# Logits matmuls in groups of forty, and the last block evacuated by VectorE with the residual added there

## The chip, the cores and the metric

One core of a Trainium2 chip. The metric is the device time of one execution in microseconds (us). Every execution shown here is fast, at a granted TensorE clock of 0.998 or more, unless it is a single look. Quoted times are medians. Ratios are the mean time of one kernel's fast runs over the mean of the kernel before's fast runs of the same rounds on the same chip, so they are not quite the ratio of the quoted medians.

## The reference

A layer norm without weights feeds two branches whose results are added to the input:

```python
xn = _layernorm(x)                       # x: 1 x 2048 x 640, bf16
return x + _A_ref(xn, wqkv, wo) + _B_ref(xn, w1, b1, w2, b2)
# A: 32 heads of 20; each position attends to 8 positions, 0, 2, .. 14 back
#    logits = sum_d q[s,d] * k[s - 2w, d];  softmax over w;  o = sum_w attn * v;  o @ wo
# B: gelu(xn @ w1 + b1) @ w2 + b2         # hidden width 1536
```

## The kernel before

The 2048 positions are worked in four chunks of 512. VectorE multiplies q with shifted k (two of the eight shifts make one product of 128 x 2 x 5 x 512). TensorE sums the 20 elements of each head with a matrix of zeros and ones, `head_of`, into the logits L. The four blocks of 128 positions go to four strips of 32 columns of the array, so each of these matmuls has the form 128*32.

```python
def do_lg(n, wp):                                   # one product: 20 matmuls
    prod = tiles["qk", n, wp]
    for t in range(KT):                             # 5
        for j in range(BPC):                        # 4 strips
            nc.tensor.matmul(L[j*H:(j+1)*H, 2*wp:2*wp+2, :], lhsT=head_of[:],
                             rhs=prod[:, :, t, j*P:(j+1)*P], ...)
    ...                                             # chunk 0: the mask
```

After the softmax, the weights `attn` (32 heads on 128 rows) are copied to the four rows that hold each head's 20 elements (4 rows of 5) by transfers into one buffer `ax`, two blocks issued from the SP queue and two from ScalarE's queue:

```python
axp = ctx.enter_context(tc.tile_pool(name="axp", bufs=1))
def do_xd(n): expand(nc.sync, n, (0, 1))
def do_xs(n): expand(nc.scalar, n, (2, 3))          # stands in ScalarE's queue
```

ScalarE empties the four PSUM buffers into which TensorE writes projections and the hidden layer. The last block of the output gets its residual by an identity matmul, and its two halves are copied out by ScalarE (lo, 512 columns) and VectorE (hi, 128 columns):

```python
if pc == 3 and n * BPC + bl == LASTB:
    srcs.append((ident[:], x_sb[:, n * BPC + bl, :]))
...
nc.scalar.copy(osb[:, 0:CH], tiles["lo", *last][:])                    # do_oclo
nc.sync.dma_start(out_sd[LASTB * P :, 0:CH], osb[:, 0:CH])
nc.vector.tensor_copy(osb[:, CH:D], tiles["hi", *last][:, 0 : D - CH]) # do_ochi
nc.scalar.dma_start(out_sd[LASTB * P :, CH:D], osb[:, CH:D])
```

A small list scheduler, run when the kernel is built, orders some 550 pieces on the engines by ranks; hand-searched offsets to these ranks stand in the table `RANK`.

## Time and profile before

| | before |
|---|---|
| time, median of 5 (range) | 218.71 us (218.47 to 218.94) |
| TensorE, VectorE, ScalarE busy | 97%, 83%, 51% of the span |
| share of TensorE in the chain that ended last | 93% |
| first projection matmul starts | 7.39 us |
| last evacuation (hi) starts | 213.65 us |
| from there to the end of the span | 3.00 us |

I call the time from the first projection to the last evacuation the stream: 213.65 - 7.39 = 206.26 us. It is the part that the change touches. In front of it are the first loads, behind it the last stores. The tail before, in the timeline:

```profile
212.64 0.59 ACT L676 CAST osb<-lo 128x512 bf16<-128x512 f32 x1 [1.89 <-issue]
...
213.25 0.36 SPq L677 DMA_DIRECT2D out_dram<-osb  x1
213.65 0.29 DVE L685 CAST osb<-hi 128x128 bf16<-128x128 f32 x1 [14.05 <-PE hi L657]
213.98 0.36 ACTq L686 DMA_DIRECT2D out_dram<-osb  x1
```

The columns are start, duration, engine, line, operation, output and input, and in brackets the idle time before and what ended it.

### The profile page before, as it was taken

How to read it: one execution, taken by the hardware profiler on the slowest of the kernel's cores; microseconds unless marked ns; L12 is line 12 of the kernel's file. 1: busy time of each engine (PE TensorE's matmuls, PEld its weight loads, DVE VectorE, ACT ScalarE, POOL GpSimd, SP SyncE). 2: the span in 40 equal slices, each digit the busy share in tenths (PEclk: the TensorE clock that was granted, in tenths of full speed). 3: DMA queues.
4: the chain of work that ended last, by engine and by line, in shares of the span. 5: the costliest groups of instructions: out<-in, count | busy, mean ns of one | idle time of the engine just before them, and what ended most of it. 6: DMA issues, size and time to landing. Idle time of an engine off the chain costs nothing.

```text
span 216.7 us, 3977 instructions
## 1 busy us (share of the span) xinstructions
PE 209.4 (97%) x1689; PEld 121.1 (56%) x1714; DVE 180.2 (83%) x169; ACT 110.6 (51%) x195; POOL 14.5 (7%) x33
## 2 busy tenths in 40 slices
PE   7899999999999999999999999999999999999994
PEld 7799855554554555555555455554544555555552
DVE  3759999988999999999899999989999999922000
ACT  3665999796757554734184625026665311341211
POOL 2000000000000000101010101011010011101121
PEclk9999999999999999999999999999999999999999
DMA  6999931907314401336020280222025222200253
GB/s 221 366 365 393 375 136 48 259 0 185 72 30 118 97 0 44 77 57 170 3 30 0 30 193 3 30 33 29 2 33 107 87 30 33 28 2 3 30 61 62
DMA packets 18761, 20.83 MB, mean 96 GB/s; under 512 B 6328, under 2 KB 15928, under 8 KB 18744
## 3 DMA queue, kind: packets, MB, share of 16 engines
q1 hardware_dynamic: 15144, 15.83, 24.7%
q0 software_dynamic: 2160, 2.46, 9.4%
q10 hardware_dynamic: 1440, 2.29, 3.1%
q8 instruction: 13, 0.21, 0.4%
q14 instruction: 4, 0.03, 0.0%
HBM read 10.00 MB, written 5.08 MB: 70 GB/s over the span
## 4 chain that ended last, share of the span: by engine, by line
PE 93%; DVE 1%; ACT 1%; DMA 1%; ACTq 1%; issue 1%; DVEq 0%
PE lo L655 27%; PE pps L455 23%; PE hps L622 22%; PE gps L472 8%; PE hi L657 8%; PE L L517 5%; DMA x_sb<-in_A_x_dram 1%; PE tp L416 1%; ACTq L584 1%; ACT L633 1%; DVE stats L375 0%; DVE stats L376 0%; ACT xnT L420 0%; ACT hT L633 0%; DVE xn L402 0%
## 5 line engine op out<-in xcount | busy, mean ns | idle before, releaser
L622 PE MATMUL hps<-xnT,w_sb 128*128 128x512 bf16 x230 | 53.2, 379 | 0.4
L655 PE MATMUL lo<-w_sb,hT 128*128 128x512 bf16 x187 | 52.9, 379 | 0.0
L505 DVE TENSOR_TENSOR prod<-qT,kT 128x2560 bf16<-128x2560 bf16 x32 | 45.4, 1483 | 0.7 <-ACT kT L490 0.7
L600 DVE TENSOR_TENSOR pv<-vT,ax 128x2560 bf16<-128x2560 bf16 x32 | 45.7, 1484 | 0.0
L657 PE MATMUL hi<-w_sb,hT 128*128 128x128 bf16 x192 | 40.3, 219 | 0.5 <-issue 0.3
L622 PEld LDWEIGHTS <-w_sb 128*128 128x128 bf16 x240 | 22.8, 98 | 26.3 <-issue 0.2
L633 ACT ACTIVATE hT<-hps,b1T 128x512 bf16<-128x512 f32 x48 | 31.4, 686 | 11.8 <-PE hps L622 9.8
L662 ACT CAST osb<-lo 128x512 bf16<-128x512 f32 x15 | 8.8, 586 | 53.8 <-PE hi L657 35.4
L609 DVE TENSOR_TENSOR pv<-pv 128x5120 bf16<-128x5120 bf16 x12 | 33.9, 2823 | 0.3
L655 PEld LDWEIGHTS <-hT 128*128 128x128 bf16 x192 | 18.7, 98 | 23.0 <-issue 1.5
L668 POOL DMA_DIRECT2D out_dram<-osb x15 | 13.1, 873 | 196.8 <-ACT osb L663 196.8
L655 PE MATMUL lo<-wo,oT 128*128 128x512 bf16 x75 | 22.1, 379 | 0.0
L657 PEld LDWEIGHTS <-hT 128*128 128x128 bf16 x192 | 18.4, 98 | 1.8
L455 PE MATMUL pps<-xnT,wv_sb 128*128 128x512 bf16 x74 | 17.3, 379 | 0.3 <-ACT hT L633 0.2
L657 PE MATMUL hi<-wo,oT 128*128 128x128 bf16 x80 | 16.9, 219 | 0.3
L455 PE MATMUL pps<-xnT,wk_sb 128*128 128x512 bf16 x74 | 16.8, 379 | 0.1
L455 PE MATMUL pps<-xnT,wq_sb 128*128 128x512 bf16 x72 | 16.7, 379 | 0.2
L490 ACT CAST vT<-pps 128x512 bf16<-128x512 f32 x15 | 8.7, 586 | 11.4 <-PE pps L455 9.4
L655 PEld LDWEIGHTS <-oT 128*128 128x128 bf16 x80 | 7.8, 98 | 9.6 <-issue 0.4
L455 PEld LDWEIGHTS <-wk_sb 128*128 128x128 bf16 x75 | 8.7, 118 | 7.3 <-issue 0.2
L455 PEld LDWEIGHTS <-wq_sb 128*128 128x128 bf16 x75 | 8.6, 118 | 7.1
L455 PEld LDWEIGHTS <-wv_sb 128*128 128x128 bf16 x75 | 8.5, 118 | 7.3 <-issue 0.5
(67 smaller groups left out, 208.9 us busy)
## 6 DMA issues: line engine op xcount, KB each, us to landing
w_sb<-in_B_w_dram SPq DMA_DIRECT2D x2, 1920.0 KB, 16.2
out_dram<-osb POOLq DMA_DIRECT2D x15, 160.0 KB, 3.4
ax<-attn SPq DMA_DIRECT2D x8, 256.0 KB, 4.9
ax<-attn ACTq DMA_DIRECT2D x8, 256.0 KB, 5.6
x_sb<-in_A_x_dram SPq DMA_DIRECT2D x3, 640.0 KB, 11.2
out_dram<-x_sb SPq DMA_DIRECT2D x3, 640.0 KB, 3.9
wq_sb<-in_A_wqkv_dram SPq DMA_DIRECT2D x1, 800.0 KB, 5.2
wk_sb<-in_A_wqkv_dram SPq DMA_DIRECT2D x1, 800.0 KB, 7.3
```

What stands on the lines that cost most here:

```text
L455: nc.tensor.matmul(ps[:], lhsT=wqkv_p[which][:, ti, to, :], rhs=xnT[:, ti, :], start=(ti == 0), stop=(ti == KT - 1),)
L472: nc.tensor.matmul(ps[:, i, :], lhsT=wqkv_p[which][:, ti, to, :], rhs=tiles["xnT", 0][:, ti, cs], start=(ti == 0), stop=(ti == KT - 1),)
L505: nc.vector.tensor_tensor(out=prod[:, i, :, :], in0=qkv_tile(n, 0)[:], in1=qkv_tile(n, 1)[:, :, off : off + CH], op=ALU.mult,)
L517: nc.tensor.matmul(L[j * H : (j + 1) * H, 2 * wp : 2 * wp + 2, :], lhsT=head_of[:], rhs=prod[:, :, t, j * P : (j + 1) * P], start=(t == 0 ...
L600: nc.vector.tensor_tensor(out=pv[:, i, :, :].rearrange("p t (j c) -> p t j c", j=BPC), in0=qkv_tile(n, 2)[:, :, off : off + CH].rearrange( ...
L609: nc.vector.tensor_tensor(out=ta[:], in0=ta[:], in1=tb[:], op=ALU.add)
L622: nc.tensor.matmul(ps[:], lhsT=w1_sb[:, ti, ft * P : (ft + 1) * P], rhs=tiles["xnT", n][:, ti, :], start=(ti == 0), stop=(ti == KT - 1),)
L633: nc.scalar.activation(hT[:], tiles["hps", n, ft][:], ACT.Gelu_apprx_tanh, bias=b1T[:, ft : ft + 1], scale=1.0)
L655: nc.tensor.matmul(lo[:], lhsT=lhs, rhs=rhs[:, 0:CH], start=first, stop=last)
L657: nc.tensor.matmul(hi[:, 0 : D - CH], lhsT=lhs, rhs=rhs[:, CH:D], start=first, stop=last)
L662: nc.scalar.copy(osb[:, 0:CH], tiles["lo", n, bl][:])
L668: nc.gpsimd.dma_start(rows, tiles["osb", n, bl][:], accum_op=ALU.add)
```

## The change

Its intent is to take work out of TensorE's stream: one group of forty logits matmuls instead of two of twenty, so that TensorE changes its tiling half as often, and no identity matmul for the last block's residual. The ranks were searched anew, so the order of all pieces differs.

```diff
-RANK = { "ad00": 178, "av2": 376.9, "f11": 47.4, ... }
+RANK = { "av2": 6.5, "f11": 4.6, "f12": 35.6, ... }
...
-            pl.add(f"lg{n}{wp}", PE, 0.65, ..., [pr, L], slack=0.8)
+            if wp % 2:
+                both = [("prod", "qk", n, wp - 1), pr]
+                pl.add(f"lg{n}{wp}", PE, 1.2, ..., both + [L], slack=0.8)
...
     def do_lg(n, wp):
-        prod = tiles["qk", n, wp]
+        for x in range(2):
+            prod = tiles["qk", n, wp - 1 + x]
+            logits(L, prod, wp - 1 + x)
...
-            if pc == 3 and n * BPC + bl == LASTB:
-                srcs.append((ident[:], x_sb[:, n * BPC + bl, :]))
...
-        nc.scalar.copy(osb[:, 0:CH], tiles["lo", *last][:])
+        nc.vector.tensor_tensor(out=osb[:, 0:CH], in0=tiles["lo", *last][:], in1=x_sb[:, LASTB, 0:CH], op=ALU.add)
...
-        nc.vector.tensor_copy(osb[:, CH:D], tiles["hi", *last][:, 0 : D - CH])
+        nc.vector.tensor_tensor(out=osb[:, CH:D], in0=tiles["hi", *last][:, 0 : D - CH], in1=x_sb[:, LASTB, CH:D], op=ALU.add)
```

## The prediction

> **What bounds the kernel now.** I read the views in this order: the page's busy shares and slices, the chain that ended last, the waits of TensorE, the timeline around one group of logits matmuls, and the timeline of the tail.
>
> The busy shares and the slices come first, because they say whether there is one bound or a sequence of them.
>
> ```profile
> PE 209.4 (97%) x1689; PEld 121.1 (56%) x1714; DVE 180.2 (83%) x169; ACT 110.6 (51%) x195; POOL 14.5 (7%) x33
> ...
> PE   7899999999999999999999999999999999999994
> ...
> PEclk9999999999999999999999999999999999999999
> ```
>
> TensorE is busy in every slice between the ramp and the tail, at a clock that is never held back. VectorE at 83% is next, and must be watched. A busy TensorE alone proves little, since it can be busy with rows that wait; the chain settles it.
>
> ```profile
> PE 93%; DVE 1%; ACT 1%; DMA 1%; ACTq 1%; issue 1%; DVEq 0%
> PE lo L655 27%; PE pps L455 23%; PE hps L622 22%; PE gps L472 8%; PE hi L657 8%; PE L L517 5%; DMA x_sb<-in_A_x_dram 1%; PE tp L416 1%; ACTq L584 1%; ACT L633 1%; DVE stats L375 0%; DVE stats L376 0%; ACT xnT L420 0%; ACT hT L633 0%; DVE xn L402 0%
> ```
>
> The chain is TensorE's own instruction stream for 93% of the span. The logits matmuls (L L517) are 5% of it. The waits of TensorE, all of them:
>
> ```profile
> PE idle L694 <- POOL ident masks.py:199: 1.6, 1, 1.6
> PE tp L416 <- DVE xn L402: 0.5, 1, 0.5
> PE hi L657 <- issue: 0.3, 2, 0.2
> PE gps L472 <- ACT xnT L420: 0.2, 1, 0.2
> PE pps L455 <- ACT hT L633: 0.2, 1, 0.2
> ```
>
> Only 0.2 us of these (pps on ACT) is waiting for another engine after the ramp; the first projection starts at 7.39 us. So from 7.39 us to the end of the matmuls at about 213.5 us the time is a sum of matmul pitches, and what this change takes out of TensorE's stream comes out of the time one for one, unless it opens a wait. From the starts in the trace, the pitches are 216 ns for 512 columns and 55.5 ns for 128.
>
> Now one group of logits matmuls, between two streams of 512 columns:
>
> ```profile
> 53.81 0.81 PE L455 MATMUL pps<-xnT,wv_sb 128*128 128x512 bf16 x3
> 54.55 0.73 PE L517 MATMUL L<-prod,head_of 128*32 128x256 bf16 x20
> 55.21 0.39 PE L655 MATMUL lo<-w_sb,hT 128*128 128x512 bf16 x1
> 55.44 0.22 PE L657 MATMUL hi<-w_sb,hT 128*128 128x128 bf16 x1
> ```
>
> The third pps matmul starts at 54.24; the first logits matmul starts 0.31 us later instead of 0.22. The lo matmul starts at 55.21. What is inside the group shows when the same timeline is cut to ever longer beginnings of another group:
>
> ```profile
> 92.74 0.29 PE L517 MATMUL L<-prod,head_of 128*32 128x256 bf16 x4
> ...
> 92.74 0.40 PE L517 MATMUL L<-prod,head_of 128*32 128x256 bf16 x8
> ...
> 92.74 0.51 PE L517 MATMUL L<-prod,head_of 128*32 128x256 bf16 x12
> ```
>
> Four matmuls (the four blocks of 32 columns of the array) run side by side, and each further round of four adds 0.11 us. A group of twenty is five rounds, 0.55 us; the rest is paid once per group, however long it is.
>
> **What the Trainium skill says.** "TensorEngine Tiling (Array Packing)", Key Properties, says that changing the tiling mode drains TensorE, while moving between tiles of one mode does not. The form 128*32 in the rows is such another mode, and the trace agrees: round to round costs 99 to 110 ns from start to start, but into and out of the mode there are holes. "TensorE: Matmul & The Clock Gate", The mechanism, has tiles in different columns starting about 4 ns apart; the trace has 3 to 4 ns between the four of a round. The same page, Back-to-back issue gap, gives about 131 ns per matmul at 512 columns as a sustained rate and 215.7 ns isolated; here the sustained pitch is 216 ns, so I use the trace. "VectorE: DVE Perf Modes", the perf-mode tier table, has tensor_tensor at one element per cycle with a PSUM operand; the trace agrees in the subtraction from the logits, 1224 ns for 1024 elements.
>
> **The change part by part.**
>
> *Groups of forty.* The fixed cost of a group, from the starts in the trace, over all sixteen groups: entering 309 - 216 = 93 ns behind 512 columns, and 149 - 55 = 94 ns behind 128; the first round takes 109 instead of 99 ns, 10; from the last round to the next foreign matmul 205 instead of 99 ns, 106; the first foreign matmul 226 instead of 216, 10. Sum 220 ns. Check: from the pps at 54.24 to the second foreign matmul at 55.44 there are 1.20 us; less 0.216 for each of the two foreign 512-column matmuls leaves 0.765, less 5 rounds of 0.109 leaves 0.22. The built order of the changed kernel has eight groups (41, 41 and six of 40 matmuls, the two of 41 with the mask), never adjacent, for sixteen. It saves 8 x 0.220 = 1.76 us. Rounds, weight loads and mask matmuls are as many as before.
>
> *Identity matmul.* Two matmuls leave the last block's chain, lo and hi from x_sb: 0.216 + 0.055 = 0.27 us, both on the path, the tail being TensorE's.
>
> *Last evacuation.* The lo half moves from ScalarE (586 ns) to VectorE. Estimate from the 1224 ns row: 1024 elements at 0.96 GHz are 1067 ns, so 157 ns fixed, and 512 elements 0.69 us. Before, the lo copy started at 212.64 and the hi copy at 213.65, 1.01 us apart; with one hi matmul fewer, 0.95 us. So VectorE has finished lo (0.69 us) before hi arrives, and nothing is added. The hi add is 128/0.96 + 157 = 0.29 us, and the copy it replaces took 0.292. The lo store is issued 0.1 us later, but the hi store still comes after it. Net zero.
>
> *The new order.* The ranks are new, so everything is reshuffled. Two things count. The transpose of b1 moves behind the load of its input, for which TensorE's loader waited 0.2 us: about -0.1. ScalarE loads activation tables 11 times instead of 9, 2 x 1283 ns more on an engine that is 51% busy.
>
> Sum: -1.76 - 0.27 - 0.1 = -2.13 us. I give 0.15 us back for small new waits in an order whose every wait I cannot check: 218.56 - 2.0 = about 216.6 us, 0.9% less.
>
> **Rivals.**
>
> *A group of forty waits for VectorE.* It needs four products before its first matmul where it needed two, and two of the four product buffers stay full until it ends. One product late by 1.4 us in every group would be 8 x 1.4 = 11 us, and the kernel would be slower. Against it: no logits matmul of the kernel before waited at all, and the order gives TensorE other work first. First group: TensorE passes 35 hps matmuls (7.6 us) and 5 transposes (0.3) after the projections that ended at 25.2, so it arrives near 33.1. VectorE began the products at 23.32; it now has one statistics block (1.0) and one scaling more ahead, so about 24.6, plus 4 x 1.40 = 30.2. Second group: TensorE 33.1 + 1.44 + 15 transposes (0.85) + 20 matmuls (4.3) = 39.7; VectorE 24.6 + 9 x 1.40 (eight products, one bias add) = 37.2. Both have over 2 us to spare. If one later group did wait, I would expect 0.3 to 1 us, not 11.
>
> *VectorE's end becomes the bound.* The last bias add (1.40 us) moves from the middle of VectorE's stream almost to its end, and its store, on which the last four accumulating stores build, goes out late. Before, VectorE idled 7.35 us before the last oT, so it can take 1.4 us more there. Two additions of 2.74 us follow the bias add, so it ends some 5.5 us before VectorE's free point of 190.8; the store takes about 3 us, and the first of those accumulating stores went out at 199 or later. It is hidden: zero.
>
> *ScalarE evacuates late.* Four PSUM buffers carry projections and hidden layer; a table load (1.28 us) at a bad place can hold TensorE. The trace shows 0.2 us of this for nine loads. Two more, fully exposed, would eat 2.6 us and leave the time where it was or 0.5 us above.
>
> *The switch is not what costs.* If the 220 ns were the loading of weights, which stays, merging would save nothing and only 0.27 us would be left (218.3). Against it: the weight loader idles 5.5 us before 15 of the groups and hardly elsewhere, which is what a drain looks like.
>
> **Range and chances.** The two sure terms give 216.5. Full exposure of one table load, or a late product or two, gives 217.6; an order a little tighter than before, which can win only the few tenths TensorE still waits, gives 215.9. I take 215.8 to 217.7. Two per cent is 4.4 us, twice what the removed work is worth, and there is no further idle time on TensorE after 7.39 us to win; 2% slower needs 6.4 us of new waits. Faster by over 2%: 0.02; within 2%: 0.95; slower: 0.03.
>
> **What would show each step right or wrong.** Right: eight groups with x40 or x41 in the timeline, the next foreign matmul 1.2 us after the first logits matmul; the loader's idle time before logits at about half of 5.5 us; no rows lo or hi from x_sb and ident; TensorE busy near 207.4 us; the lo add near 0.69 us and done before the hi add begins. Wrong: a wait of an L row on prod in TensorE's waits; pps or hps waiting on ACT rows for more than 1 us; groups that last 1.5 us (the cost scales with matmuls); or a first projection that no longer starts at 7.4 us, which I took as unchanged.

## More of the kernel before

```profile
123.89 2.30 ACTq L584 DMA_DIRECT2D ax<-attn  x2
126.23 0.59 ACT L490 CAST vT<-pps 128x512 bf16<-128x512 f32 x1 [2.00 <-issue]
```

Two issues hold ScalarE's queue for 2.30 us, and the evacuation behind them waits. TensorE did not wait for it there.

## The result, and the profile after

The changed kernel takes 218.34 us (217.94 to 218.39, five runs) against 218.71: ratio 0.998, 95% interval 0.9965 to 0.9995. The gain is real and tiny, 0.4 us where 2.0 were predicted, and the time lies outside the predicted range. Busy shares and chain after:

```profile
PE 208.2 (96%) x1689; PEld 122.4 (57%) x1712; DVE 181.1 (84%) x170; ACT 111.4 (51%) x196; POOL 14.5 (7%) x33
...
PE 59%; DVE 32%; ACTq 2%; ACT 2%; issue 2%; DMA 1%; DVEq 0%
```

TensorE is busy 1.2 us less, and it no longer carries the whole chain: a third of the span now leads through VectorE, and ScalarE's queue (ACTq) has 2%. Each group of forty, here one between streams of 512 columns, is as predicted:

```profile
94.98 0.81 PE L458 MATMUL pps<-xnT,wk_sb 128*128 128x512 bf16 x3
95.72 1.28 PE L534 MATMUL L<-prod,head_of 128*32 128x256 bf16 x40
96.93 0.41 PE L458 MATMUL pps<-xnT,wk_sb 128*128 128x512 bf16 x1
```

The foreign matmul comes 1.21 us after the first of the forty, as the prediction asked. From the starts in the trace, entering still costs 309 ns instead of 216 and leaving 205 instead of 99. The weight loader's idle time in front of logits, in its view of waits before and after, halves with the number of groups:

```profile
PEld L517 <- issue: 5.5, 15, 0.4
```

```profile
PEld L534 <- issue: 3.0, 8, 0.4
```

What came in its place is in the waits of TensorE after the change:

```profile
PE pps L458 <- ACT vT L493: 0.8, 1, 0.8
...
PE pps L458 <- ACT hT L640: 0.5, 1, 0.5
```

From start to start these two cost 0.93 us (at 131 us) and 0.69 us (at 55 us). The waits view shows less, since it counts from the modelled ends of the matmuls. Around the one at 131 us the timeline shows three engines:

```profile
122.70 5.69 DVE L607 TENSOR_TENSOR pv<-vT,ax 128x2560 bf16<-128x2560 bf16 x4
122.92 4.48 PE L458 MATMUL pps<-xnT,wv_sb 128*128 128x512 bf16 x20
...
128.43 2.32 ACTq L591 DMA_DIRECT2D ax<-attn  x2
...
130.79 2.05 ACT L493 CAST vT<-pps 128x512 bf16<-128x512 f32 x4 [6.93 <-issue]
131.43 1.02 PE L458 MATMUL pps<-xnT,wv_sb 128*128 128x512 bf16 x4 [0.77 <-ACT vT L493]
```

TensorE fills the four PSUM buffers (20 matmuls) by 127.4 us. ScalarE should empty them, but in its queue the issues of the third chunk's expansion stand first. They may not start before VectorE has read the old contents of `ax`, at 128.4, and then take 2.3 us. Before the change the same issues left at 123.89, because VectorE was 4.5 us earlier there. The wait at 55 us stands behind the first chunk's pair of issues, with a table load of ScalarE between (first in ScalarE's view, then in that of all engines):

```profile
50.85 2.44 ACTq L591 DMA_DIRECT2D ax<-attn  x2
...
53.94 1.28 ACT L640 ACT_TABLE_LOAD   x1
55.23 1.27 ACT L640 ACTIVATE hT<-hps,b1T 128x512 bf16<-128x512 f32 x2
```

```profile
54.21 1.24 PE L458 MATMUL pps<-xnT,wq_sb 128*128 128x512 bf16 x5
...
55.97 1.24 PE L458 MATMUL pps<-xnT,wq_sb 128*128 128x512 bf16 x5 [0.52 <-ACT hT L640]
```

The tail after:

```profile
212.50 0.69 DVE L681 TENSOR_TENSOR osb<-lo,x_sb 128x512 bf16<-128x512 f32 x1 [16.09 <-PE lo L660]
...
213.21 0.35 SPq L682 DMA_DIRECT2D out_dram<-osb  x1
213.39 0.29 DVE L690 TENSOR_TENSOR osb<-hi,x_sb 128x128 bf16<-128x128 f32 x1 [0.20 <-PE hi L662]
213.71 0.36 ACTq L693 DMA_DIRECT2D out_dram<-osb  x1
```

The stream is 213.39 - 7.63 = 205.76 us, only 0.50 shorter. The first projection started 0.24 us later, and the end, after the hi add, is 0.15 us longer. The store of the lo half, from issue to landing, before and after (last column, us; the hi store, which lands last, takes 1.69 instead of 1.53):

```profile
out_dram<-osb SPq DMA_DIRECT2D x1, 128.0 KB, 1.7
```

```profile
out_dram<-osb SPq DMA_DIRECT2D x1, 128.0 KB, 2.0
```

### The profile page after: what moved, and what is told of

The parts are those of the page before. It is cut to its first block, busy times and chain, and to the rows that moved or that the text cites. A ratio compares the mean times of both kernels' runs of the same rounds, so it can differ in the third digit from the quotient of the medians.

```text
span 216.5 us, 3974 instructions
## 1 busy us (share of the span) xinstructions
PE 208.2 (96%) x1689; PEld 122.4 (57%) x1712; DVE 181.1 (84%) x170; ACT 111.4 (51%) x196; POOL 14.5 (7%) x33
## 4 chain that ended last, share of the span: by engine, by line
PE 59%; DVE 32%; ACTq 2%; ACT 2%; issue 2%; DMA 1%; DVEq 0%
PE lo L660 19%; PE hps L629 18%; DVE pv L607 10%; DVE prod L508 9%; PE gps L475 8%; PE pps L458 5%; PE hi L662 5%; DVE pv L616 5%; PE L L534 2%; ACTq L591 2%; DVE ssum L569 2%; DMA x_sb<-in_A_x_dram 1%; DVE attn L581 1%; DVE m L547 1%; PE tp L419 1%
## 5 line engine op out<-in xcount | busy, mean ns | idle before, releaser
L629 PE MATMUL hps<-xnT,w_sb 128*128 128x512 bf16 x232 | 54.5, 379 | 0.5
L458 PE MATMUL pps<-xnT,wv_sb 128*128 128x512 bf16 x73 | 16.6, 379 | 0.8 <-ACT vT L493 0.8
L681 DVE TENSOR_TENSOR osb<-lo,x_sb 128x512 bf16<-128x512 f32 x1 | 0.7, 692 | 16.1 <-PE lo L660 16.1
L378 DVE BATCH_NORM_STATS2 stats<-x_sb 128x6 f32<-128x320 bf16 x16 | 7.4, 463 | 7.6 <-DMA x_sb<-in_A_x_dram 7.5
```

What stands on the lines that cost most here:

```text
L458: nc.tensor.matmul(ps[:], lhsT=wqkv_p[which][:, ti, to, :], rhs=xnT[:, ti, :], start=(ti == 0), stop=(ti == KT - 1),)
L629: nc.tensor.matmul(ps[:], lhsT=w1_sb[:, ti, ft * P : (ft + 1) * P], rhs=tiles["xnT", n][:, ti, :], start=(ti == 0), stop=(ti == KT - 1),)
```

## The experiments

Theory A: the work removed from TensorE is worth what was predicted, and the new order gives it back, by ScalarE's transfer issues standing in front of PSUM evacuations. Rivals: B, groups of forty make their own waits in any order; C, a switch is cheap and the small gain is all there is; D, which arose later, the new order makes VectorE the bound whatever ScalarE issues. A fifth, E, concerns the last block alone and stands in the expectation of b_grp_sp.

To separate order from work, I pinned the order: the names of all pieces in a list, which the kernel emits instead of asking the scheduler. The list of the b runs is the order that the scheduler of before gives, without lg00, lg02, .. where groups are merged; a_xs2 and a_twenty have the changed kernel's order but for the pieces named; a_sp needs no list, since its scheduler gives that order. No pinned copy was run without a further edit. In the table, "stream" and "hi to end" are from the profiled execution; labels starting with b have the order of before, those with a the order of after.

| run | time, median us | ratio (95%) | first projection | stream | hi to end |
|---|---|---|---|---|---|
| before | 218.71 | | 7.39 | 206.26 | 3.00 |
| before_again | 218.66 (one look) | | 7.65 | 206.23 | 2.97 |
| after | 218.34 | 0.998 (0.9965-0.9995) | 7.63 | 205.76 | 3.15 |
| b_grp | 217.39 | 0.9946 (0.9933-0.9959) | 7.51 | 204.88 | 2.98 |
| b_last | 219.73 | 1.0053 (1.002-1.0085) | 7.70 | 205.93 | 3.49 |
| b_last_again | 218.83 | 1.0004 (0.999-1.0018) | 7.61 | 206.09 | 3.19 |
| b_both | 217.27 | 0.9938 (0.9926-0.995) | 7.82 | 204.55 | 3.19 |
| a_xs2 | 218.39 | 0.9992 (0.998-1.0004) | 7.69 | 205.61 | 3.13 |
| a_sp | 217.19 | 0.9922 (0.991-0.9935) | 8.04 | 204.14 | 3.20 |
| a_twenty | 219.59 | 1.0039 (1.0027-1.0051) | 7.44 | 207.16 | 3.12 |
| b_both_sp | 217.03 | 0.9919 (0.9906-0.9931) | 7.65 | 203.98 | 3.68 |
| b_grp_sp | 217.35 | 0.9941 (0.9927-0.9954) | 7.47 | 204.91 | 2.94 |
| b_one_sp | 217.22 | 0.9947 (0.9926-0.9968) | 7.94 | 204.09 | 3.33 |

All outputs are right.

**b_grp: only the groups, in the order of before.**

```diff
 # order of before; lg00, lg02, .. dropped, lg01, lg03, .. do both products
-        nc.vector.tensor_tensor(out=osb[:, 0:CH], ..., op=ALU.add)
+        nc.scalar.copy(osb[:, 0:CH], tiles["lo", *last][:])     # last block as before
```

> The order of the kernel before, pinned piece by piece; only the logits groups are merged (each pair of twenties runs as one forty at the place of the second). Theory A (the merge is worth 8 x 0.22 us; the changed kernel gives it back because its new order puts ScalarE's issues of the weight-expansion transfers in front of PSUM evacuations): 1.3 to 1.8 us below before, no new TensorE wait over 0.4 us. Theory B (groups of forty make their own waits in any order): 0 to 0.6 us below before, with TensorE waits of over 1 us. Theory C (a switch costs little, the change of 0.2 to 0.4 us seen is all of it): 0.2 us below, with no waits.

Measured: 0.9946, which is 1.2 us below before; the stream is 1.38 us shorter. It has one new wait, for a kT evacuation by ScalarE near 97 us (0.3 us in the waits, 0.42 from start to start); with it the groups have saved 1.38 + 0.42 = 1.80 us, where 1.76 were predicted. The wait stands behind a pair of expansion issues too (94.01 to 96.36 us), and b_grp_sp below, without such issues on ScalarE, does not have it. The time falls just short of the range that theory A gave; C is out, and so is B.

**b_last: only the last block.**

```diff
 # order and groups of twenty of before; do_o, do_oclo and do_ochi of after
```

> The order and groups of twenty of the kernel before; only the last block is changed (no identity matmul, residual added by VectorE). Theory A and B: 0.27 us below before, the lo add near 0.69 us and finished before the hi add. Theory C, in which the last block gives the whole gain seen: the same 0.2 to 0.3, so this run only sizes that term.

Measured: no gain but 1.0053, with times from 218.71 to 221.44, while before on the same chip stayed within 0.4 us. The stream is 0.33 us shorter, as expected, but the end after the hi add grew by 0.49 us. Both theories had missed that. I repeated it.

> The run of the last block alone, repeated, because its five times spread over 2.7 us while before's on the same chip spread over 0.4. If the spread is its own: again runs of 220 and more. If it was chance: 218.3 to 218.8. In either case, from the start of the hi add to the end of the last store about 0.2 us or more longer than before's 1.85 us, since the two last stores are issued 0.50 instead of 0.73 us apart.

Measured: 1.0004, 218.42 to 219.48. The slowest runs of the first try did not come back, a wider spread than that of before did. Stream 0.17 us shorter, end 0.19 longer. No gain of the last block's change is shown.

**b_both: both parts in the order of before.**

> The order of before with both parts of the change. Theory A: the two add up, 1.6 to 2.0 us below before (near 216.8), that is 1.2 to 1.7 us below the changed kernel, though its instructions are the same and only the order differs. Theory B and C: within 0.4 us of the changed kernel.

Measured: 0.9938, 217.27 us: 1.4 us below before and 0.9 (by the ratios) to 1.1 (by the medians) below the changed kernel, which has the same pieces in another order. That is a little less than theory A's range: the last block brings nothing in time, and the kT wait of b_grp is there too (0.45 us). It is far from what B and C say.

**a_xs2: one piece of the changed kernel moved.**

```diff
-  ... xs2 xd2 o101 o102 pc320 ... pc324 ...
+  ... xd2 o101 o102 pc320 ... pc324 xs2 ...      # in ScalarE's queue behind the vT copies
```

> The changed kernel with one piece moved: ScalarE issues its two expansion transfers of the third chunk behind its evacuations of that chunk's next projections instead of in front of them. Theory A: TensorE's wait of 0.77 us for the vT evacuation near 131 us goes and about 0.8 to 0.9 us of time with it (near 217.4). Theory B and C: the wait is not what ends the kernel, or reappears elsewhere: within 0.2 us of the changed kernel.

Measured: 0.9992, no gain over the changed kernel. A miss for theory A as I had put it. The wait at 131 us did go, but another of 0.7 us (0.82 from start to start) came up at 168, and the stream is only 0.15 us shorter:

```profile
163.47 4.48 PE L653 MATMUL hps<-xnT,w_sb 128*128 128x512 bf16 x20
...
164.71 3.10 ACTq L615 DMA_DIRECT2D ax<-attn  x2
...
167.86 1.27 ACT L664 ACTIVATE hT<-hps,b1T 128x512 bf16<-128x512 f32 x2 [3.45 <-DVE pv L640]
168.60 0.59 PE L653 MATMUL hps<-xnT,w_sb 128*128 128x512 bf16 x2 [0.65 <-ACT hT L664]
```

It is the same pattern one chunk later: four buffers full, two issues of together 3.1 us in front of the evacuation. In the changed kernel TensorE had come to this place late enough not to notice. Taking away one such wait only moves it to the next; so I took away all of them.

**a_sp: the changed kernel with all expansions issued from the SP queue.**

```diff
 def do_xs(n):
-    expand(nc.scalar, n, (2, 3))
+    expand(nc.sync, n, (2, 3))
```

> The changed kernel, with ScalarE's half of the weight-expansion transfers issued from the SP queue instead, so that ScalarE's queue never stands behind an issue of 2.3 us or behind the wait for the expansion buffer. Theory A, sharpened (the new order lets these issues delay ScalarE's evacuations, first the last kT of chunk 1, by which VectorE runs some 4 us late from 54 us on, and then vT, for which TensorE waits): VectorE's first pv moves from 61.0 us to below 60, both TensorE waits (0.5 and 0.8 us) go, and the time falls by 0.9 to 1.5 us against the changed kernel, to about 217.1. Theory D (the order itself, not ScalarE's issues, makes VectorE the bound): within 0.3 us of the changed kernel, with the waits moved elsewhere as in the run that moved one issue.

Measured: 0.9922, 217.19 us, within what theory A gave. The stream falls by 1.62 us against the changed kernel, to 204.14, and that is the two waits, 0.93 + 0.69: set side by side, weight load by weight load, the two traces part at 55 and 131 us and nowhere else in the stream by more than 0.06 us. It is 2.12 us below before, where the prediction had summed 2.13. The agreement is partly luck: a_sp also lacks a wait of 0.14 us that before has at 53 us and that the sum did not count. The waits of TensorE and the chain:

```profile
PE idle L701 <- POOL ident masks.py:199: 1.5, 1, 1.5
PE tp L419 <- DVE xn L405: 0.6, 1, 0.6
PE gps L475 <- ACT xnT L423: 0.5, 1, 0.5
```

```profile
PE 95%; DMA 1%; DVE 1%; ACT 0%; issue 0%
```

All that is left lies ahead of the first projection. One part of what I expected failed: VectorE's first pv did not come earlier (61.17 us instead of 60.97), because it now waits for the last of the expansions, which lands at 61.15 us instead of 59.02. VectorE is as late as in the changed kernel, and here that costs TensorE nothing. ScalarE's vT copies still wait for VectorE, which reads the old v until about then:

```profile
127.94 2.05 ACT L493 CAST vT<-pps 128x512 bf16<-128x512 f32 x4 [4.36 <-DVE pv L607]
```

They start at 127.94 instead of 130.79, and that is early enough for TensorE. What cost the time was the issues in between, not the gate before them. The table load of the wait at 55 us is here too (at 52.17 us), without a wait. Theory D is out.

**a_twenty: the changed kernel's order with groups of twenty.**

```diff
 # order of after, with lg00, lg02, .. put one TensorE piece ahead of lg01, lg03, ..
```

> The changed kernel's order and last block with groups of twenty: each first product's matmuls stand one TensorE piece ahead of the second's. If a switch costs 0.22 us and TensorE is the bound throughout, 1.76 us slower than the changed kernel. Theory A: part of it hides in the waits that the changed kernel has anyway (the four groups between 55 and 130 us lie before a wait of 0.93 us that ends at a time set by VectorE), so 0.7 to 1.2 us slower, and that wait shrinks to nearly nothing. Theory C (switches are cheap): under 0.3 us slower.

Measured: 1.0039, against 0.998 for the changed kernel about 1.3 us slower, just over theory A's range and well under 1.76; the stream is 1.40 us longer. The eight further switches cost 1.86 in this order (four of them 0.24 each instead of 0.22, since the first projection matmul behind the logits takes 248 ns), the wait at 131 us shrinks from 0.93 to 0.23, and the wait at 55 us, which I had not counted, grows by 0.24 to 0.93: 1.86 - 0.70 + 0.24 = 1.40. So the merge did pay in the changed kernel too, and part of it ran into a wait that ended at the same time anyway.

**b_both_sp: before's order, both parts, SP issues.**

> The order of before with both parts of the change and with the expansions issued from the SP queue: if ScalarE's issues cost TensorE anything in that order too (its trace shows waits of 0.1 and 0.45 us behind ScalarE), 0.2 to 0.5 us below the run without the move, near 216.9; otherwise equal to it.

Measured: 0.9919, 217.03 us (four runs), beside b_both 0.2 us less by the medians and 0.4 by the ratios, on another chip, and 0.57 us less in the stream, the shortest of all. No TensorE wait is left after the first projection. The end after the hi add is 3.68 us in this profile, the longest of all and 0.49 longer than b_both's, so that in this execution most of the stream's gain was lost again.

**b_grp_sp and b_one_sp: what the last block is worth.** The first is b_both_sp with the last block of before; the second stores both halves of the last block at once:

```diff
 def do_oclo():
-    nc.sync.dma_start(out_sd[LASTB * P :, 0:CH], osb[:, 0:CH])
 def do_ochi():
-    nc.scalar.dma_start(out_sd[LASTB * P :, CH:D], osb[:, CH:D])
+    nc.sync.dma_start(out_sd[LASTB * P :, :], osb[:])
```

> The order of before, groups of forty, expansions issued from the SP queue, and the last block as it was before (identity matmul, lo copied by ScalarE). Theory E (the last block's change gains 0.27 us in TensorE's stream and loses as much or more after the last evacuation, because the lo store leaves later and the two last stores run into one another): from hi evacuation to the end 3.0 us as in before instead of 3.1 to 3.7, the lo store lands 1.7 us after its issue instead of 2.0 to 2.5, TensorE's stream 0.27 us longer than in the run with both parts and SP issues, and the time within 0.2 us of it (217.0) on either side. If the last block's change is worth its 0.27 us after all: 217.3.

Measured: 0.9941, 217.35 us. The end is 2.94 us and the lo store lands 1.7 us after its issue, both as expected. The time lies where it was expected if the last block's change is worth its 0.27 us after all (217.3), and not where theory E put it. But the stream is longer than b_both_sp's by 0.93 and not by 0.27: in this execution TensorE also waited for VectorE's oT (0.36 us from start to start) and for loads at 10 and 12 us (0.23). So the time does not decide between the two last blocks. The two ran on different chips besides.

> Both parts, before's order, SP issues, but the last block's two halves go out in one store of 640 columns after the hi add. Theory E: without a second store to run into, hi evacuation to end is near 3.0 to 3.2 us and the same from run to run, time 216.7 to 217.0. If the longer tail has another cause: as the run with two stores, 3.2 to 3.7 us, or worse by the 0.4 us that the bigger store starts later.

Measured: 217.22 us, 0.9947, five runs from 217.02 to 217.48 and one of 218.59. End 3.33 us. One store in place of two doesn't win the tail back, and the time is over what theory E gave. Nor does it rule out that two stores disturb each other: the one store of 160 KB landed after 1.8 us, sooner than the 128 KB of any run with two stores 0.5 us apart (2.0 to 2.5), but it leaves with all its bytes only after the hi add.

**before_again: a second profile of before.**

> The kernel before, unchanged, for a second profile: how much the start of the first projection (7.39 us in the first profile, 7.4 to 8.0 in the others) and the end differ between two executions of the same program. Nothing in the change touches the start, so the first projection should start anywhere in 7.4 to 8.0 here too, and hi evacuation to end should be 3.0 again.

Measured: first projection at 7.65, stream 206.23, end 2.97. The stream repeats within 0.03 us; the start doesn't, and its 0.24 us between the two first profiles is no effect of the change.

## Why the prediction was right or wrong

*TensorE's stream bounds the kernel.* Right for before, and right for the changed kernel once its waits are gone (a_sp: 95% of the chain). For the changed kernel itself it was no longer true.

*A switch costs 0.22 us, eight fewer save 1.76.* Right. The entry, exit and round times are the same in the groups of forty, b_grp shows 1.38 in the stream with a wait of 0.42 beside it, and a_twenty closes the sum from the other side. One reading was not quite so: the first foreign matmul takes 226 ns behind most of the sixteen groups, but 247 to 248 behind three of them (at 38, 93 and 100 us). The rival that the switch is not what costs is dead.

*The identity matmul is worth 0.27 us.* Right in the stream (0.33 and 0.17 in the two runs of b_last as a whole, 0.27 at the place of the two matmuls in both).

*Last evacuation: net zero.* Wrong, by about as much as the identity matmul was worth. The durations were right (the lo add took 692 ns, predicted 0.69; the hi add 0.29; the 0.96 GHz agrees with the trace of before, where 1024 elements take 1224 ns and 128 take 292, so 1.04 ns each), and lo was done before hi. What failed is that I ended the sum at the evacuation. In the four profiles with lo on ScalarE the end after the hi evacuation is 2.94 to 3.00 us, in the eight with a lo add on VectorE and two stores it is 3.12 to 3.68, and the lo store takes 2.0 to 2.5 us instead of 1.7. The end grows by what the hi store, which lands last, takes longer: 1.67 to 2.23 us instead of 1.49 to 1.53. The lo store leaves 0.1 us later and the hi store 0.5 instead of 0.73 us after it. That the stores get in each other's way is my argument, not shown: the run with one store did not get the 3.0 us back. Nor is the larger spread of some runs explained (over 1 us in b_last_again, but also in b_grp_sp, which has the old last block, and under 0.4 in b_both and a_sp, which have the new one).

*"I give 0.15 us back for small new waits."* This is the step that failed. The new waits are worth 1.62 us and not 0.15: the two waits behind ScalarE's evacuations measure 0.93 and 0.69 us, and just that much comes back in the stream when ScalarE's issues are moved (a_sp). So the sum closes: 2.13 - 1.62 = 0.51 (the stream fell by 0.50), less 0.15 at the end, and 0.4 us were measured (with the luck named at a_sp in the 2.13). The prediction's own sign of being wrong, pps waiting on ACT rows for more than 1 us, came true (0.8 + 0.5 in the waits view), and TensorE is busy 208.2 us instead of near 207.4. I had checked VectorE's arrival before the first two groups, and those did not wait; I had not checked what stands in front of ScalarE's evacuations. The order, which I had before me, shows the third chunk's expansion ahead of four vT copies, and the profile of before shows what such a pair of issues costs, 2.30 us.

*Rival: ScalarE evacuates late.* The right engine with the wrong cause and a wrong weight. I looked at two more table loads, allowed 2.6 us if both were fully exposed, and put only one of them, at most, into the range. It was the transfer issues, and a table load (1.28 us) only in the wait at 55 us, where it stands behind such a pair. The one wait of before that I put down to table loads (0.2 us in the waits, 0.14 from start to start) stands behind such a pair as well, 2.13 us of issues at 49.18, and it goes when the issues move to SP (b_grp to b_grp_sp). So the trace of before already showed the cause.

*Rival: a group of forty waits for VectorE.* Did not happen; no L row waits, and TensorE came to the first two groups at 33.13 and 39.89 us, where 33.1 and 39.7 were predicted.

*Rival: VectorE's end becomes the bound.* Hidden, as predicted, but VectorE's free time before the last oT shrank from 7.35 to 1.05 us, much more than the 1.4 us I had moved there. That VectorE ran late from 54 us on may be why; no run tests it.

*The first projection starts at 7.4 us, unchanged.* It scatters from 7.39 to 8.04 us over the profiles, 7.39 to 7.65 for one and the same kernel. That is too much to ignore where a change is worth 2 us in all.

## What to carry to other kernels

When TensorE is the bound, work taken out of it brings the next engine's fixed times nearer: a place where it used to arrive late can become a wait, so check what stands in each evacuating engine's queue ahead of the evacuations, not only what that engine adds up to. Keep transfer issues off an engine that has to empty PSUM; here one word (`nc.sync` for `nc.scalar`) was worth three times the change itself in the new order, and 0.4 or 0.1 us in the order of before (b_both_sp, b_grp_sp). The long issues are not ScalarE's own: where its pair left 3.5 us after that of SP (a_xs2, at 132 us) the two took 0.55 and 0.62 us, and with all four on SP (a_sp) the third and fourth took 1.2 to 1.8 us. A new order is a change of its own: to judge a part, pin the order and change the part alone.

## What the Trainium skill lacked or had wrong

- "TensorEngine Tiling (Array Packing)", Key Properties: it says that a mode switch drains TensorE, without a figure. Here going into a 128*32 group and back costs some 220 ns beyond its rounds, 94 of them on entering, 106 on leaving and 10 each in the first round and the first foreign matmul.
- "TensorE: Matmul & The Clock Gate", Back-to-back issue gap: about 131 ns per matmul at 512 columns sustained in a real kernel. Here the sustained pitch is 216 ns in all kernels, at a full granted clock.
- "DMA: Bandwidth & Descriptors", Issuing engines are not separate DMA queues: the sequencer's time to start a transfer is called usually small beside the transfer. Here two expansion issues hold ScalarE's queue for 2.0 to 3.1 us when SP issues two more at the same time, where one such transfer lands 4.3 to 7.5 us after its issue in the changed kernel; single issues there took 0.54 to 0.65 us on SP and 0.56 to 1.75 on ScalarE, and 0.54 to 1.83 on SP where SP issues all four (a_sp).
- No page that I read says that two stores issued 0.5 us apart both land later: the one of 128 KB landed after 2.0 to 2.5 us and the one of 32 KB after 1.7 to 2.2 in all eight such profiles, against 1.7 and 1.5 us in the four where they were 0.73 us apart. In the eight, VectorE and not ScalarE wrote the first half, so the cause stays open.
